# Windowed attention and MLP on one core: one block group of four middle tiles as seven products, with the next batch's casts moved one tile ahead

## Chip, cores and metric

The kernel runs on one core of a Trainium2 chip. The metric is the device time of one execution in microseconds (us), lower is better; it is given as the median of several runs.

## What is computed

There are 8 batches of 8 heads, 576 positions and head dimension 64. Each position attends to the positions at most 32 away; the result goes through a two-layer MLP (512 to 2048 to 512, tanh form of GELU). Inputs and output are float32.

```python
scores = 1/sqrt(64) * q @ k.T          # masked where |i - j| > 32
attn   = softmax(scores)
x      = (attn @ v) as (8 * 576 tokens, 8 heads * 64)
h      = x @ w_in                      # 4608 x 2048
out    = (0.5 * h * (1 + tanh(c * (h + 0.044715 * h**3)))) @ w_out
```

## The kernel before

**Tiles and batches.** The 4608 tokens are worked through in nine tiles of 512 (`t` = 0 to 8, loop at L930). A tile has two parts on TensorE (PE). The *in part* multiplies by `w_in`: 16 blocks of 128 hidden features, each four matmuls of 512 columns (`ffn_in`, L558, matmul L577), and ScalarE (ACT) takes each block through GELU (`gelu`, L583) into `gT`. The *out part* multiplies by `w_out` as seven products of half-size matrices in place of eight (Strassen-Winograd, `ffn_out`, L732, 112 matmuls of 256 columns, L751). The seven products need sums of parts of `gT`, which VectorE (DVE) makes during the in part (`sums`, L686, four instructions for each quarter), and DVE combines the seven results (L762 to L789). Products 0, 2, 4 and 6 share one PSUM bank and products 1, 3 and 5 another, so that product n+2 can start only when the DVE instruction that reads product n has run.

**Attention inside the out part.** While the out part of tile `t` runs, the attention of batch `b = t + 1` is threaded into it. `PLAN` (L46; `PLAN_1` for tile 1) says at which of the 112 matmuls a step is issued: `s` scores of a pair of heads and their exponential, `m` the mask on DVE, `v` the product with the values and the inverse of the sum, `x` the write of the result into `xT`, the transposed MLP input. Group 4 of a batch (its last positions, written -1 for the batch before) uses the "tails" `qt`, `kt`.

**Getting a batch ready.** Queries and keys are loaded in float32 by DMAs that SyncE (SP) issues (`load_qk`, L180: one transfer for q, four for k, two for the tails). DVE casts them to float16 (`turn_queries`, L408, cast L410; `turn_keys`, L416, cast L419; `turn_tails`, L425), and SP issues transposing DMAs into `QT`, `KT` and `KL`. From tile 3 on these casts stand at the head of the in part of the tile in whose out part the batch is attended: batch `t+1` is cast at the beginning of tile `t`, and the loads of batch `t+2` are issued after that. Values go by POOL's queue (`load_v`, L213), released by a one-element copy (L989) that waits for `KL`, and DVE copies them into a second arrangement (`pair_v`, L222).

**The last two tiles.** Tiles 7 and 8 already do two groups of four blocks, named A and B, of their in part as seven products each (`in_product`, L616; matmuls of 256 columns at L629). `in_x` (L606) makes four differences of parts of `xT`, `in_w` (L591) four combinations of `w_in` (once), and `in_mixed` (L632) walks the string `MIX` (L62): a number is a plain block, `A3` or `B3` a product, `s`, `c` and `g` the copy, addition and GELU that follow, `t` and `u` the two halves of `sums`.

**What sets the order.** The order is written out by hand and each engine takes its own instructions in that order. A DVE instruction that waits for data holds back all that follows it on DVE.

The lines that the change and the steps below touch are `PLAN`, `MIX`, `PLAN_1`, the pools of the raw tiles (`rawp`, L109), `load_qk`, `load_tails` (L205), `turn_queries`, `turn_keys`, `turn_tails`, `in_w`, `in_x`, `in_product`, `in_mixed`, `ffn_out` and the main loop.

Of the kernel before, what the change touches and what calls it, by code (L numbers as in the profile page):

```python
# [36 lines left out]
def cut(b):  # L37
# [8 lines left out]
PLAN = {7: "s0@0 s1@1 v-1", 16: "m0 m1 x-1", 33: "s2@0 v0@1 v1", 36: "m2", 44: "x0", 50: "x1",  # L46
        62: "s3@0 s4@1 v2", 66: "m3", 80: "x2", 84: "m4", 91: "v3", 112: "x3"}
# [14 lines left out]
MIX = ("3 g3 A0 s0A B0 s0B 12 g12 A2 B2 cA00 cB00 A1 s1A gA00 A4 B1 s1B gB00 B4 t0 u0 13 g13 A3 s3A B3 s3B 14 g14 "  # L62
       "cA11 cB11 A5 gA10 B5 gB10 gA11 gB11 A6 B6 cA01 cB01 15 gA01 gB01 t1 t2 g15 t3 u1 u2 u3").split()
UNITS = {"A": 1, "B": 2}

PLAN_1 = {12: "s0@0 s1@1 s2", 16: "m0 m1", 36: "m2", 56: "s-1@0 v0@1 v1", 62: "m-1 x0", 64: "x1",
          78: "s3@0 v2 v-1@1", 79: "m3", 88: "x2", 91: "x-1", 97: "v3 s4@1", 112: "x3 m4"}
# [5 lines left out]

RING = 1536
# [4 lines left out]
def kernel(  # L79
# [29 lines left out]
    rawp = ctx.enter_context(tc.tile_pool(name="rawp", bufs=2))  # L109
# [27 lines left out]
    def load_early(b):  # L137


        qr = rawp.tile([128, H, 256], FP32, name="qr")  # L140
        kr = rawp.tile([128, H, 256], FP32, name="kr")
        raws[b] = [qr, kr, None]

        def qk(h0, queues=(nc.sync, nc.sync)):
            for src, dst, queue in zip((q, k), (qr, kr), queues):
                queue.dma_start(
                    dst[:, h0:h0 + 2, :],
                    src[b, h0:h0 + 2, 0:512, :].rearrange("h (p j) d -> p h (j d)", j=4))
# [29 lines left out]
        return qk, tails, vs  # L178

    def load_qk(b):  # L180


        if b == 3:
            qr = raws[3]
        else:
            qr = rawp.tile([128, H, 256], FP32, name="qr")
            load_q(b, qr)
        kr = rawp.tile([128, 4, H, 64], FP32, name="kr")
        if b > 3:
            qt = tailp.tile([16, H, 256], FP32, name="qt", tag="vt")  # L190
            kt = tailp.tile([64, H, 64], FP32, name="kt", tag="tr")
            raws[b] = (qr, kr, qt, kt)
        else:
            raws[b] = [qr, kr, tailp.tile([128, H, 64], FP32, name="tr", tag="tr"), None]
        for c in range(4):
            nc.sync.dma_start(kr[:, c, :, :],
                              k[b, :, 128 * c:128 * c + 128, :].rearrange("h p d -> p h d"))
        load_tails(b, nc.sync)
        if b == 3:
            load_vr(3)  # L200
# [4 lines left out]
    def load_tails(b, queue):  # L205
        if b > 3:
            queue.dma_start(raws[b][2], q[b, :, 512:576, :].rearrange("h (p j) d -> p h (j d)", j=4))
# [194 lines left out]
    def load_vr(b):  # L402
        vr = vrs[b] = rawp.tile([128, 4, H, 64], FP32, name="qr")
# [4 lines left out]
    def turn_queries(b, src, dst, p0, p1):  # L408
# [4 lines left out]
        nc.sync.dma_start_transpose(QTs[b].rearrange("d r j p -> d (r j) p")[:, :, p0:p1],  # L413
                                    dst.rearrange("p r j h d -> p (r j h d)"))

    def turn_keys(b):  # L416
        k16, kr = halfs[b][1], raws[b][1]
        for pr in range(NPAIR):
# [6 lines left out]
    def turn_tails(b):  # L425
        qt, kt = raws[b][2:4]
        qt16 = hp.tile([16, NPAIR, 4, 2, 64], FP16, name="qt16", tag="qt16")
        kt16 = hp.tile([64, NPAIR, 2, 64], FP16, name="kt16", tag="t16")
        turn_queries(b, qt, qt16, 128, 144)
# [4 lines left out]
    def open_and_turn(b):  # L434
        cast_open(b)
        turn_queries(b, raws[b][0], halfs[b][0], 0, 128)
# [154 lines left out]
    def in_w(eng, unit, *which):  # L591
# [14 lines left out]
    def in_x(t):  # L606
# [3 lines left out]
        xc = hp.tile([128, 4, 2, 256], FP16, name="xc", tag="q16" if t % 2 else "k16")  # L610
# [21 lines left out]
    def in_mixed(t):  # L632
        if "A" not in mixed:
            mixed["A"] = rawp.tile([128, 3, 512], FP32, name="sa", tag="qr")
            mixed["B"] = rawp.tile([128, 3, 512], FP32, name="sb", tag="kr")

        place = {"00": (0, "b"), "01": (1, "c"), "11": (2, "c")}
        for step in MIX:
            kind, rest = step[0], step[1:]
            if kind in UNITS:  # L640
                in_product(kind, int(rest))
# [16 lines left out]
            elif kind in "tu":  # L658
                sums(t, int(rest), slice(0, 2) if kind == "t" else slice(2, 4))
# [72 lines left out]
    def ffn_out(t, i):  # L732

        n, blk, f = i // 16, i // 8 % 2, i % 8
        if n == 1 and t >= NT - 2:
            blk, f = divmod(i % 16, 6) if i % 16 < 12 else (i // 2 % 2, 6 + i % 2)
# [28 lines left out]
        elif n == 2:  # L765
            nc.vector.tensor_copy(C11, py)
            if end:
# [162 lines left out]
    for t in range(NT):  # L930
        b = t + 1
        att = b < B
        if t:
# [50 lines left out]
        if t and b + 1 < B:  # L984
            load_qk(b + 1)
        ods = {}
        for i in range(113 if t else 65):
# [8 lines left out]
            for act in plan.get(i, "").split():  # L996
# [61 lines left out]
            if t in (3, 4) and i == 52:  # L1058
                in_w(nc.vector, "B", *((1, 2) if t == 3 else (3, 4)))
# [12 lines left out]
            elif t and i < 112:  # L1072
                ffn_out(t, i)
# [36 lines left out]
```

## Time and profile before

| what | value |
|---|---|
| median of 3 runs | 296.62 us (296.36 to 296.83) |
| the profiled execution | 296.65 us, span 294.6 us |
| PE busy | 285.9 us, 97% of the span |
| DVE busy | 212.4 us, 72% |
| ACT busy | 196.5 us, 67% |
| POOL busy | 88.8 us, 30% |
| tiles 3, 4, 5, 6 (start of one in part to the next) | 30.42, 30.48, 30.42, 30.41 us |
| tiles 7 and 8 (8 to the last matmul) | 26.40, 26.2 us |

The span runs from the first to the last instruction; the time has some 2 us more around it. Busy PE time counts pipelined matmuls, so a full PE is not PE at its peak: the distance from the start of one matmul to the next says more. In a timeline the columns are start, duration, engine, line, operation, output from input with shapes, count, and in square brackets the idle time before the instruction with what ended it.

### The profile page before, as it was taken

What the parts mean: (1) busy time and instruction counts of PE and PEld (TensorE: products, weight loads), DVE (VectorE), ACT (ScalarE), POOL (GpSimd) and SP (SyncE); (2) the same over time, 40 slices, a digit from 0 to 9 for tenths busy, and PEclk for the clock granted to TensorE, in tenths of its full rate; (3) what the DMA queues carried; (4) which work ended last, traced back from release to release, by engine and by line L of the source; (5) the groups of instructions that cost most, each with busy time, mean ns of one, the idle gap of its engine ahead of it and who ended that gap; (6) DMA issues with size and microseconds to landing.
All of it is one profiled execution on the core that took longest, in us unless ns stands there. A gap on an engine that the chain in (4) does not pass through costs nothing.

```text
span 294.6 us, 7286 instructions
## 1 busy us (share of the span) xinstructions
PE 285.9 (97%) x2945; PEld 192.7 (65%) x2945; DVE 212.4 (72%) x467; ACT 196.5 (67%) x315; POOL 88.8 (30%) x143
## 2 busy tenths in 40 slices
PE   8889999999999999999999999999999999999993
PEld 3535545547765687568755885588558867887783
DVE  4755477998897667858796878686957877865762
ACT  5965877777677874787667776796669558706800
POOL 4445335004228713205250615050800050025000
PEclk9999999999999999999999999999999999999998
DMA  7999998999999998999999999899691040004013
GB/s 229 275 380 396 359 305 196 254 186 203 248 229 202 251 202 188 113 139 245 162 212 94 246 157 191 116 245 154 117 190 7 0 118 28 2 26 120 0 47 99
DMA packets 114392, 51.02 MB, mean 173 GB/s; under 512 B 98471, under 2 KB 110247, under 8 KB 114102
## 3 DMA queue, kind: packets, MB, share of 16 engines
q1 hardware_dynamic: 89460, 38.67, 62.4%
q0 software_dynamic: 23776, 10.83, 23.4%
q10 hardware_dynamic: 1122, 1.06, 1.1%
q8 instruction: 23, 0.38, 0.6%
q14 instruction: 11, 0.09, 0.1%
HBM read 36.70 MB, written 9.44 MB: 157 GB/s over the span
## 4 chain that ended last, share of the span: by engine, by line
PE 85%; DVE 5%; DMA 5%; issue 1%; SPq 1%; ACT 1%; POOL 0%; DVEq 0%
PE mm L751 32%; PE ph L577 17%; PE mm L577 16%; PE ps_s L468 4%; PE pu L629 3%; DMA kr<-in_k_dram 3%; PE mm L723 2%; DMA wst<-in_moe_w_in_dram 2%; PE py L723 2%; PE ps_d L495 2%; PE ps_o L505 2%; DVE t L684 2%; DVE s L694 1%; PE mm L629 1%; PE ps_od L495 1%; PE ps_od L505 1%
## 5 line engine op out<-in xcount | busy, mean ns | idle before, releaser
L577 PEld LDWEIGHTS <-w_in 128*128 128x128 f16 x512 | 57.4, 113 | 49.8 <-POOL w_in L250 1.5
L577 PE MATMUL ph<-xT,w_in 128*128 128x512 f16 x256 | 64.5, 379 | 0.6 <-POOL w_in L250 0.6
L577 PE MATMUL mm<-xT,w_in 128*128 128x512 f16 x256 | 64.1, 379 | 0.0
L585 ACT ACTIVATE gT<-mm 128x512 f16<-128x512 f32 x60 | 35.6, 598 | 33.3 <-PE mm L577 32.7
L713 POOL DMA_DIRECT2D out_dram<-y x55 | 32.8, 605 | 82.4 <-DVE y L780 75.3
L751 PEld LDWEIGHTS <-s 128*128 128x128 f16 x512 | 49.3, 98 | 7.1 <-DVE s L694 0.6
L751 PE MATMUL mm<-t,s 128*128 128x256 f16 x376 | 45.2, 273 | 0.2 <-DVE y L764 0.2
L694 DVE TENSOR_TENSOR s<-gT 128x512 f16<-128x512 f16 x64 | 27.5, 430 | 19.1 <-ACT gT L585 18.9
L751 PEld LDWEIGHTS <-gT 128*128 128x128 f16 x384 | 36.2, 98 | 6.4
L585 ACT ACTIVATE gT<-ph 128x512 f16<-128x512 f32 x58 | 32.4, 604 | 10.9 <-PE ph L577 10.9
L481 ACT ACTIVATE pe<-ps_s 128x960 f16<-128x960 f32 (+1 forms) x31 | 29.5, 975 | 13.2 <-PE ps_s L468 13.1
L751 PE MATMUL mm<-w_out,gT 128*128 128x256 f16 x256 | 32.6, 273 | 0.0
L104 ACT ACT_TABLE_LOAD x18 | 23.1, 1283 | 2.2 <-issue 1.9
L530 ACT ACTIVATE lt<-ps_d 128x480 f32<-128x480 f32 (+2 forms) x28 | 15.6, 556 | 10.4 <-PE ps_d L495 6.9
L531 ACT ACTIVATE lt<-lt 128x480 f32<-128x480 f32 (+3 forms) x36 | 21.1, 585 | 1.1
L490 DVE TENSOR_TENSOR pe<-pe,band 128x960 f16<-128x960 f16 x28 | 18.5, 680 | 2.0 <-ACT pe L481 1.9
L505 PEld LDWEIGHTS <-V 128*64 128x64 f16 x520 | 13.7, 111 | 5.5 <-DVE V L226 1.5
L751 PE MATMUL mm<-t,gT 128*128 128x256 f16 x128 | 16.1, 273 | 0.0
L694 DVE TENSOR_TENSOR s<-s,gT 128x512 f16<-128x512 f16 x32 | 14.0, 436 | 1.1
L216 POOL DMA_DIRECT2D V<-in_v_dram x16 | 14.3, 908 | 1.1 <-PE ps_s L468 0.4
L751 PE MATMUL mm<-w_out,s 128*128 128x256 f16 x120 | 14.6, 273 | 0.0
L540 DVE TENSOR_TENSOR xT<-ps_o,lt 128x480 f16<-128x480 f32 (+5 forms) x26 | 13.4, 535 | 1.6 <-PE ps_o L505 1.6
(149 smaller groups left out, 390.3 us busy)
## 6 DMA issues: line engine op xcount, KB each, us to landing
kr<-in_k_dram SPq DMA_DIRECT2D x31, 256.0 KB, 10.2
qr<-in_q_dram SPq DMA_DIRECT2D x6, 1024.0 KB, 5.9
wst<-in_moe_w_in_dram SPq DMA_DIRECT2D x8, 512.0 KB, 6.6
wst<-in_moe_w_out_dram SPq DMA_DIRECT2D x2, 1024.0 KB, 10.5
wst<-in_moe_w_out_dram SPq DMA_DIRECT2D x4, 512.0 KB, 7.4
qr<-in_v_dram SPq DMA_DIRECT2D x8, 256.0 KB, 6.5
V<-in_v_dram POOLq DMA_DIRECT2D x16, 128.0 KB, 8.5
qr<-in_q_dram SPq DMA_DIRECT2D x7, 256.0 KB, 7.3
```

What stands on the lines that cost most here:

```text
L104: nc.scalar.add_instruction(mybir.InstLoadActFuncSet(name=nc.get_next_instruction_name(), act_func_set_id=which, ins=[], outs=[]))
L216: nc.gpsimd.dma_start(V[:, c, :, :], v[b, :, 128 * c:128 * c + 128, :].rearrange("h p d -> p h d"))
L481: nc.scalar.activation(pe, ps[:, :, 0:w], AF.Exp, scale=SCALE)
L490: nc.vector.tensor_tensor(pe, pe, m.rearrange("k (o j) p -> k o j p", o=1).broadcast_to(list(pe.shape)), op=ALU.mult)
L505: nc.tensor.matmul(o[64 * h:64 * h + 64, cols].rearrange("d (j p) -> d j p", j=4)[:, :, p0 - q0:p1 - q0], Vs[b % 2][:, slot, 2 * pr + h, : ...
L530: nc.scalar.activation(lt[:, 0:n], d[:, 0:n], AF.Ln)
L531: nc.scalar.activation(lt[:, 0:n], lt[:, 0:n], AF.Exp, scale=-1.0)
L577: nc.tensor.matmul(ph, w_cols[:, dc, fc // 4, fc % 4, :], xT[:, dc, t * 512 % RING:t * 512 % RING + 512], start=(dc == 0), stop=(dc == 3))
L585: nc.scalar.activation(gTs[t][:, fc, :], phs[fc], AF.Gelu_apprx_tanh)
L694: nc.vector.tensor_tensor(dst, x, y, op=op)
L713: eng.dma_start(out_v[b, j, q0 + p:q0 + p + e, cols], yo[m:m + e, cols])
L751: nc.tensor.matmul(pys["apart"][:, 0:256] if apart else py[:, blk, :], lhsT, wino[w][:, f, :], start=(new and i % (8 if one else 16) == 0) ...
```

## The change

- Tiles 3 to 6 do group B of their in part (blocks 8 to 11) as seven products, by a new string `MIX_1`; the other twelve blocks stay plain. `in_w` for B runs in the in part of tile 2 (before: in the out parts of tiles 3 and 4); `in_x` runs at the head of each tile from 3 on.
- The casts of queries and keys of batch `t+2` move from the head of tile `t+1` into the out part of tile `t` (new steps `a0` to `a3` and `b0` to `b3` in `PLAN`), from tile 2 on. The tails' casts stay in the in part (`f0`, `f1` in `MIX_1`).
- The loads of batch `t+2` are issued inside the in part of tile `t` (step `load`), for batch 4 at block 10 of tile 2.
- In `PLAN`, `v1` moves from 33 to 36; in `PLAN_1`, `v1`, `m-1` and `s4` move; in tile 1 the transposes of the tails move from block 8 to block 6.
- In tiles 7 and 8 the sums S4 of three quarters (`z1 z2 z3`) move from the end of the in part to behind the copy of product 2; the order of product 1 changes; tile 7's last attention group moves from 40 and 66 to 16 and 40; in tile 8 the last four matmuls of product 1 change places with the first four of product 2.
- The raw tiles get fixed buffers in place of rotating ones.

```diff
-PLAN = {7: "s0@0 s1@1 v-1", 16: "m0 m1 x-1", 33: "s2@0 v0@1 v1", 36: "m2", 44: "x0", 50: "x1",
-        62: "s3@0 s4@1 v2", 66: "m3", 80: "x2", 84: "m4", 91: "v3", 112: "x3"}
+PLAN = {7: "s0@0 s1@1 v-1", 16: "m0 m1 x-1", 33: "s2@0 v0@1", 36: "m2 v1", 44: "x0 a0", 50: "x1 a1 a2 a3",
+        62: "s3@0 s4@1 v2 b0 b1", 66: "m3", 80: "x2 b2", 84: "m4 b3", 91: "v3", 112: "x3"}
...
-MIX = ("3 g3 A0 s0A B0 s0B 12 g12 A2 B2 cA00 ...
-       "cA11 cB11 A5 gA10 B5 gB10 gA11 gB11 A6 B6 cA01 cB01 15 gA01 gB01 t1 t2 g15 t3 u1 u2 u3").split()
+MIX = ("3 g3 A0 s0A B0 s0B A2 B2 12 g12 cA00 ...
+       "cA11 cB11 A5 gA10 B5 gB10 gA11 gB11 A6 B6 cA01 cB01 15 gA01 gB01 t1 t2 g15 t3 w1 w2 w3").split()
+MIX_1 = ("f0 3 B0 g3 s0B 4 B2 cB00 B1 s1B load f1 g4 5 g5 6 g6 t0 u0 B3 s3B gB00 pair B4 7 g7 cB11 gB11 12 g12 t1 u1 B5 gB10 B6 cB01 gB01 13 g13 14 g14 t2 u2 15 g15 t3 u3").split()
...
+PARTS = {"t": slice(0, 2), "u": slice(2, 4), "w": slice(2, 3), "z": slice(3, 4)}
+LONE = 3
...
+    def turn_query(b, pr):
+        src, dst = raws[b][0], halfs[b][0]
+        nc.vector.tensor_copy(
+            dst[:, pr, :, :, :].rearrange("p j h d -> p h j d"),
+            src[:, 2 * pr:2 * pr + 2, :].rearrange("p h (j d) -> p h j d", j=4))
+        if pr == NPAIR - 1:
+            nc.sync.dma_start_transpose(QTs[b].rearrange("d r j p -> d (r j) p")[:, :, 0:128],
+                                        dst.rearrange("p r j h d -> p (r j h d)"))
+
+    def turn_keys(b, prs=range(NPAIR)):
...
         if n == 1 and t >= NT - 2:
-            blk, f = divmod(i % 16, 6) if i % 16 < 12 else (i // 2 % 2, 6 + i % 2)
+            blk, f = divmod(i % 16, 4) if i % 16 < 8 else (i // 2 % 2, i // 4 % 4 * 2 + i % 2)
...
         elif n == 2:
             nc.vector.tensor_copy(C11, py)
+            if t >= NT - 2:
+                for step in "z1 z2 z3".split():
+                    sums(t, int(step[1]), PARTS[step[0]])
...
             elif att:
-                if b > 3:
-                    open_and_turn(b)
-                turn_keys(b)
-                if b > 3:
-                    turn_tails(b)
+                if t >= LONE:
+                    in_x(t)
+                if b == 3:
+                    turn_keys(b)
...
-            for fc in range(begun, NF if t < NT - 2 else 0):
+            elif t >= LONE:
+                in_mixed(t)
+            for fc in range(begun, NF if t < LONE else 0):
...
+                if t == 2 and fc == 10:
+                    load_qk(4)
+                if t == LONE - 1 and fc in (8, 9, 10, 11):
+                    in_w(nc.vector, "B", (8, 9, 10, 11).index(fc) + 1)
...
+                elif kind in "ab":
+                    if b + 1 < B:
+                        if kind + str(g) == "a0":
+                            cast_open(b + 1)
+                        turn_query(b + 1, g) if kind == "a" else turn_keys(b + 1, (g,))
...
-                ffn_out(t, i)
+                ffn_out(t, i if t < NT - 1 or not 28 <= i < 36 else i + 4 if i < 32 else i - 4)
```

More of the change, by code (lines that the diff above doesn't have):

```diff
@@ L56 @@
           59: "p0@0 p2@1 x0 x1", 60: "e4 x2 x3", 61: "c1"}
-MIX = ("3 g3 A0 s0A B0 s0B 12 g12 A2 B2 cA00 cB00 A1 s1A gA00 A4 B1 s1B gB00 B4 t0 u0 13 g13 A3 s3A B3 s3B 14 g14 "
-       "cA11 cB11 A5 gA10 B5 gB10 gA11 gB11 A6 B6 cA01 cB01 15 gA01 gB01 t1 t2 g15 t3 u1 u2 u3").split()
+MIX = ("3 g3 A0 s0A B0 s0B A2 B2 12 g12 cA00 cB00 A1 s1A gA00 A4 B1 s1B gB00 B4 t0 u0 13 g13 A3 s3A B3 s3B 14 g14 "
+       "cA11 cB11 A5 gA10 B5 gB10 gA11 gB11 A6 B6 cA01 cB01 15 gA01 gB01 t1 t2 g15 t3 w1 w2 w3").split()
+MIX_1 = ("f0 3 B0 g3 s0B 4 B2 cB00 B1 s1B load f1 g4 5 g5 6 g6 t0 u0 B3 s3B gB00 pair B4 7 g7 cB11 gB11 12 g12 t1 u1 B5 gB10 B6 cB01 gB01 13 g13 14 g14 t2 u2 15 g15 t3 u3").split()
 UNITS = {"A": 1, "B": 2}
-PLAN_1 = {12: "s0@0 s1@1 s2", 16: "m0 m1", 36: "m2", 56: "s-1@0 v0@1 v1", 62: "m-1 x0", 64: "x1",
-          78: "s3@0 v2 v-1@1", 79: "m3", 88: "x2", 91: "x-1", 97: "v3 s4@1", 112: "x3 m4"}
+PARTS = {"t": slice(0, 2), "u": slice(2, 4), "w": slice(2, 3), "z": slice(3, 4)}
+PLAN_1 = {12: "s0@0 s1@1 s2", 16: "m0 m1", 36: "m2", 56: "s-1@0 v0@1", 60: "v1 m-1", 62: "x0", 64: "x1",
+          78: "s3@0 v2 v-1@1", 79: "m3", 88: "x2", 91: "x-1", 97: "v3", 101: "s4@1", 112: "x3 m4"}
 PAIR_1 = {38: slice(0, 4), 50: slice(4, 8)}
@@ L108 @@
     big = ctx.enter_context(tc.tile_pool(name="big", bufs=1))
-    rawp = ctx.enter_context(tc.tile_pool(name="rawp", bufs=2))
+    rawp = ctx.enter_context(tc.tile_pool(name="rawp", bufs=1))
     hp = ctx.enter_context(tc.tile_pool(name="hp", bufs=1))
@@ L137, in load_early @@
     def load_early(b):
-        qr = rawp.tile([128, H, 256], FP32, name="qr")
-        kr = rawp.tile([128, H, 256], FP32, name="kr")
+        qr = rawp.tile([128, H, 256], FP32, name="qr", tag=f"q{b}")
+        kr = rawp.tile([128, H, 256], FP32, name="kr", tag=f"k{b}")
         raws[b] = [qr, kr, None]
@@ L185, in load_qk @@
         else:
-            qr = rawp.tile([128, H, 256], FP32, name="qr")
+            qr = rawp.tile([128, H, 256], FP32, name="qr", tag="q0")
             load_q(b, qr)
-        kr = rawp.tile([128, 4, H, 64], FP32, name="kr")
+        kr = rawp.tile([128, 4, H, 64], FP32, name="kr", tag="k1" if b == 3 else "k0")
         if b > 3:
-            qt = tailp.tile([16, H, 256], FP32, name="qt", tag="vt")
-            kt = tailp.tile([64, H, 64], FP32, name="kt", tag="tr")
-            raws[b] = (qr, kr, qt, kt)
+            raws[b] = [qr, kr]
         else:
@@ L197, in load_qk @@
                               k[b, :, 128 * c:128 * c + 128, :].rearrange("h p d -> p h d"))
-        load_tails(b, nc.sync)
+        if b < 5:
+            load_tails(b, nc.sync)
         if b == 3:
@@ L206, in load_tails @@
         if b > 3:
+            raws[b] += [tailp.tile([16, H, 256], FP32, name="qt", tag="vt"),
+                        tailp.tile([64, H, 64], FP32, name="kt", tag="tr")]
             queue.dma_start(raws[b][2], q[b, :, 512:576, :].rearrange("h (p j) d -> p h (j d)", j=4))
@@ L402, in load_vr @@
     def load_vr(b):
-        vr = vrs[b] = rawp.tile([128, 4, H, 64], FP32, name="qr")
+        vr = vrs[b] = rawp.tile([128, 4, H, 64], FP32, name="vr", tag="q1")
         for c in range(4):
@@ L406, in load_vr, with turn_queries @@
                               v[b, :, 128 * c:128 * c + 128, :].rearrange("h p d -> p h d"))
-    def turn_queries(b, src, dst, p0, p1):
+    def turn_queries(b):
+        src = raws[b][2]
+        dst = hp.tile([16, NPAIR, 4, 2, 64], FP16, name="qt16", tag="qt16")
         for pr in range(NPAIR):
@@ L412, in turn_queries @@
                 src[:, 2 * pr:2 * pr + 2, :].rearrange("p h (j d) -> p h j d", j=4))
-        nc.sync.dma_start_transpose(QTs[b].rearrange("d r j p -> d (r j) p")[:, :, p0:p1],
+        nc.sync.dma_start_transpose(QTs[b].rearrange("d r j p -> d (r j) p")[:, :, 128:144],
                                     dst.rearrange("p r j h d -> p (r j h d)"))
-    def turn_keys(b):
+    def turn_query(b, pr):
[7 more added lines that the diff above has]
+    def turn_keys(b, prs=range(NPAIR)):
         k16, kr = halfs[b][1], raws[b][1]
-        for pr in range(NPAIR):
+        for pr in prs:
             nc.vector.tensor_copy(k16[:, pr, :, :, :], kr[:, :, 2 * pr:2 * pr + 2, :])
@@ L423, in turn_keys, with turn_key_tails @@
                     k16[:, pr - 1:pr + 1, :, :, :].rearrange("p r c h d -> p (r c h d)"))
-    def turn_tails(b):
-        qt, kt = raws[b][2:4]
-        qt16 = hp.tile([16, NPAIR, 4, 2, 64], FP16, name="qt16", tag="qt16")
+    def turn_key_tails(b):
+        kt = raws[b][3]
         kt16 = hp.tile([64, NPAIR, 2, 64], FP16, name="kt16", tag="t16")
-        turn_queries(b, qt, qt16, 128, 144)
         nc.vector.tensor_copy(kt16.rearrange("p r h d -> p (r h d)"), kt.rearrange("p h d -> p (h d)"))
@@ L435, in open_and_turn @@
         cast_open(b)
-        turn_queries(b, raws[b][0], halfs[b][0], 0, 128)
+        for pr in range(NPAIR):
+            turn_query(b, pr)
     groups = {}
@@ L595, in in_w @@
         if (unit, "s") not in mixed:
-            halves = [(rawp if unit == "A" else yp).tile([128, 2, 2, 2, 128], FP16, name="wc" + unit + str(x),
-                                                         tag=("qr", "kr")[x] if unit == "A" else "yo") for x in range(2)]
-            mixed[unit, "s"] = [half[:, x] for half in halves for x in range(2)]
+            if unit == "A":
+                wc = rawp.tile([128, 4, 2, 2, 128], FP16, name="wcA", tag="q0")
+                mixed[unit, "s"] = [wc[:, x] for x in range(4)]
+            else:
+                mixed["xw"] = rawp.tile([128, 2, 4, 2, 256], FP16, name="xw", tag="k1")
+                mixed[unit, "s"] = [mixed["xw"][:, 1, x].rearrange("p d (h c) -> p d h c", h=2) for x in range(4)]
         S1, S2, S3, S4 = mixed[unit, "s"]
@@ L609, in in_x @@
         B11, B12, B21, B22 = (xT[:, d:d + 2, pos + c:pos + c + 256] for d in (0, 2) for c in (0, 256))
-        xc = hp.tile([128, 4, 2, 256], FP16, name="xc", tag="q16" if t % 2 else "k16")
+        xc = mixed["xw"][:, 0] if t < NT - 2 else \
+            hp.tile([128, 4, 2, 256], FP16, name="xc", tag="q16" if t % 2 else "k16")
         T1, T2, T3, T4 = (xc[:, x] for x in range(4))
@@ L614, in in_x, with in_product @@
             nc.vector.tensor_tensor(dst, a, b, op=ALU.subtract)
-    def in_product(unit, n):
+    def in_product(unit, n, alone):
         a, w, new = WINO[n]
         if n == 0:
-            phs[unit, "a"] = psO.tile([128, 512], FP32, name="pu", tag="O") if unit == "A" else bank(1)
+            phs[unit, "a"] = psO.tile([128, 512], FP32, name="pu", tag="O") if unit == "A" or alone else bank(1)
         elif n in (2, 4):
             which = "b" if n == 2 else "c"
-            if unit == "A":
+            if unit == "A" or alone:
                 phs[which] = psS.tile([128, 2, 512], FP32, name="pu2", tag="S1" if n == 2 else "S0")
@@ L632, in in_mixed @@
     def in_mixed(t):
-        if "A" not in mixed:
-            mixed["A"] = rawp.tile([128, 3, 512], FP32, name="sa", tag="qr")
-            mixed["B"] = rawp.tile([128, 3, 512], FP32, name="sb", tag="kr")
+        if "B" not in mixed:
+            mixed["B"] = rawp.tile([128, 3, 512], FP32, name="sb", tag="q1")
+        if t == NT - 2:
+            mixed["A"] = rawp.tile([128, 3, 512], FP32, name="sa", tag="k0")
         place = {"00": (0, "b"), "01": (1, "c"), "11": (2, "c")}
-        for step in MIX:
+        for step in MIX if t >= NT - 2 else MIX_1:
             kind, rest = step[0], step[1:]
-            if kind in UNITS:
-                in_product(kind, int(rest))
+            if step == "pair":
+                pair_v(t + 1, nc.vector.tensor_copy)
+            elif step == "load":
+                if t + 2 < B:
+                    load_qk(t + 2)
+            elif step == "f0":
+                turn_queries(t + 1)
+            elif step == "f1":
+                turn_key_tails(t + 1)
+                if t + 2 < B:
+                    load_tails(t + 2, nc.sync)
+            elif kind in UNITS:
+                in_product(kind, int(rest), t < NT - 2)
             elif kind == "s":
@@ L657, in in_mixed @@
                 nc.scalar.activation(gTs[t][:, fc, :], phs[fc], AF.Gelu_apprx_tanh)
-            elif kind in "tu":
-                sums(t, int(rest), slice(0, 2) if kind == "t" else slice(2, 4))
+            elif kind in PARTS:
+                sums(t, int(rest), PARTS[kind])
             else:
@@ L958 @@
                     nc.sync.dma_start(raws[2][4], v[2, :, 512:S, :].rearrange("h p d -> p h d"))
-                    raws[3] = rawp.tile([128, H, 256], FP32, name="qr")
+                    raws[3] = rawp.tile([128, H, 256], FP32, name="qr", tag="q0")
                     load_q(3, raws[3])
@@ L963 @@
                     cast_v(2, fc - 6)
+                if t == 1 and fc == 6:
+                    trans_tails(1, psO.tile([128, 8, 128], FP16, name="pt", tag="O"))
                 if t == 1 and fc == 8:
-                    trans_tails(1, psO.tile([128, 8, 128], FP16, name="pt", tag="O"))
                     cast_tails(2, nc.scalar.copy)
@@ L974 @@
                                 copy_q=nc.scalar.copy)
-                if t > 1 and fc == 8 and att:
+                if t == 2 and fc == 8:
                     pair_v(b, nc.vector.tensor_copy)
-        plan = PLAN_0 if not t else PLAN_1 if t == 1 else PLAN if att else {40: "v-1", 66: "x-1"} if t == B - 1 else {}
+                if t == 2 and fc == 10:
+                    load_qk(4)
+                if t == LONE - 1 and fc in (8, 9, 10, 11):
+                    in_w(nc.vector, "B", (8, 9, 10, 11).index(fc) + 1)
+        plan = PLAN_0 if not t else PLAN_1 if t == 1 else PLAN if att else {16: "v-1", 40: "x-1"} if t == B - 1 else {}
         def group(g):
@@ L983 @@
             load_table(exp_set)
-        if t and b + 1 < B:
+        if t == 1:
             load_qk(b + 1)
@@ L1057 @@
                 in_x(t + 1)
-            if t in (3, 4) and i == 52:
-                in_w(nc.vector, "B", *((1, 2) if t == 3 else (3, 4)))
             if t == NT - 3 and i in (52, 86):
```

## Prediction

> **What bounds the kernel now.** I read the page's busy line and the chain of waits first, then the table of windows by tile, then the timelines of PE, DVE and SP around the places that the change touches. The busy line and the engine shares of the chain:
>
> ```profile
> PE 285.9 (97%) x2945; PEld 192.7 (65%) x2945; DVE 212.4 (72%) x467; ACT 196.5 (67%) x315; POOL 88.8 (30%) x143
> PE 85%; DVE 5%; DMA 5%; issue 1%; SPq 1%; ACT 1%; POOL 0%; DVEq 0%
> ```
>
> PE is the bound, and from tile 3 to 6 it never idles (30.42 busy of 30.42 us in the windows). So there a change is worth what it takes from PE, unless something newly makes PE wait. Two lines of the chain, of a plain in part and of tile 8's products (start, duration, what, count):
>
> ```profile
> 154.72 1.73 PE mm L577 x8
> ...
> 269.13 1.75 PE pu L629 x16
> ```
>
> A 512-column matmul costs 0.216 us from start to start, a 256-column one 0.109.
>
> **Seven products, tiles 3 to 6.** Removed for each tile: 4 blocks x 4 matmuls x 0.216 = 3.45 us. Added: 7 products x 4 x 0.109 = 3.06. Gain 0.39 a tile, **1.6 us** in four.
> A rule of the Trainium skill speaks against it: "TensorE: Matmul & The Clock Gate", section "Back-to-back issue gap", gives 81 ns sustained for 128 columns and 131 for 512; between them 256 columns would be some 98 (an estimate), and 28 x 98 against 16 x 131 ns would lose 0.65 us a tile, 2.6 in all. The rows above measure both shapes in this kernel and decide.
>
> What comes with it lies on DVE and ACT. DVE in the in part gains `in_x` (1.5 us in tile 7, 238.11 to 239.65), one copy and three additions of 0.6 each, 3.9 us, and loses the query and key casts, 1.47 + 1.49: net 0.9, against 3.1 us in which DVE idled there in tile 4 (0.62 + 0.62 + 1.90 before the sums). ACT gains two copies of 0.58 against some 3 us of idle between GELUs (0.27 each). Without these covers the 0.9 and 1.2 us would delay the sums or GELUs by as much a tile. The product's bank is read by DVE between B0 and B1 (0.7 us, with block 4 and B2, 1.3 us of PE, between): no wait. I cost them at nothing.
>
> **Casts in the out part, tiles 3 to 5.** Eight casts of 0.37 us join DVE. The tight place is ahead of L771, which product 5 waits for. In tile 4 there stood 1.2 us of `in_w` and 0.39 idle; now a0 to b1, 6 x 0.37 = 2.2. L771 ends 0.6 later, at 171.9, and product 5 begins at 172.18: 0.3 us left. Nothing again, at most 0.2 a tile. On SP, QT and KT now go before the loads, KL behind q and k; KL is first needed by `s4`, values a tile later. In tile 4 of before, loads issued at 131.23 were cast at 146.8 and 148.3 without a wait, 17.1 us for k at most; now they are issued some 5.8 us into the in part and k is cast at 24.1, 18.3 us later: on time, with little proved slack.
>
> **Tile 2 is different.** Its out part now casts batch 4, a whole in part sooner, but its loads do not go out sooner: SP issues back to back. SP and DVE in tiles 2 and 3 (start, duration, engine, line), and the landing of the k transfers issued from 95.5 on:
>
> ```profile
> 93.67 2.14 SPq L203 DMA_DIRECT2D qr<-in_q_dram  x1
> 95.86 13.13 SPq L196 DMA_DIRECT2D kr<-in_k_dram  x4
> 109.09 3.01 SPq L207 DMA_DIRECT2D qt<-in_q_dram  x1
> ```
>
> ```profile
> L196 SPq DMA_DIRECT2D kr<-in_k_dram x4: 1109/3064/5760, 95.9 to 106.6; - x4
> ...
> DMA to landing us min/median/max: 12.7/12.7/12.7
> ```
>
> ```profile
> 106.27 0.66 DVE L540 TENSOR_TENSOR xT<-ps_od,lt 128x480 f16<-128x480 f32 x1 [0.44 <-ACT lt L531]
> 106.89 0.69 DVE L766 COPY y<-mm 128x512 f32<-128x512 f32 x1
> 107.49 0.65 DVE L540 TENSOR_TENSOR xT<-ps_o,lt 128x480 f16<-128x480 f32 x1
> 109.80 0.69 DVE L771 TENSOR_TENSOR y<-mm,y 128x512 f32<-128x512 f32 x1 [1.66 <-PE mm L751]
> ...
> 118.00 1.57 DVE L419 CAST k<-kr 128x512 f16<-128x512 f32 x4
> ```
>
> `kr` is issued in four parts, the last at 106.6 (SP is not idle from 49 us to there, and the changed kernel's SP order up to these loads is the same). Emitting `load_qk(4)` at block 10 moves it past nothing on SP. The third part, issued at 102.8, lands 12.7 later, at 115.5; each k cast reads all four parts. The fourth lands after that and no later than 118.0, where the cast began without a recorded wait. In the new order b0 stands after x1 and a1 to a3, at about 109.2 (108.1 + 3 x 0.37), and waits on DVE until k lands. Behind it are queued b1, L771, m3, L774, x2, and for L771 waits product 5:
>
> ```profile
> 109.37 2.14 PE L751 MATMUL mm<-t,s 128*128 128x256 f16 x18
> 111.34 1.36 PE L751 MATMUL mm<-t,gT 128*128 128x256 f16 x11
> ```
>
> Product 5 started at 111.34. Now it starts at landing + 2 x 0.37 + 0.69. For the landing I take 117.2, near the 118.0 row, a little less because the output stores that ran beside it from 114.95 now come later. 117.2 + 1.43 = 118.6: **PE waits 7.3 us** (5.6 to 8.1 by the two rows). q is no such case: a0 stands at 106.9, and casting q is at most some 0.5 late.
>
> PE then also loses its clock. After the last matmul (290.0) the granted clock fell:
>
> ```profile
> 290.00:294.60 4.60, 0.00 (x0) 0.00 (x0) 0.42 (x1) 0.00 (x0) 0.00 (x0) 0.81 0.39 104
> ```
>
> 0.81 (the eighth column) in 4.6 us means half speed for 1.75, so it fell 2.85 us after the last matmul. A wait of 7.3 is longer. The way back is seen at the start:
>
> ```profile
> 1.26 3.59 PE L288 MATMUL spin<-KT 128*128 128x512 f16 x8 [1.26 <-DVE KT L283]
> 4.65 0.62 PE L382 MATMUL pt<-idn,q 128*128 128x128 f16 x4
> ```
>
> Eight matmuls in 3.39 us, 0.424 each, where 8 x 0.216 = 1.73 would do: **1.7 us lost** on resuming. Bounds: 0 (clock kept) to 3.4 (twice that slow stretch); I take the row.
>
> **Tail, tiles 7 and 8.** In tile 8, L764 stood behind six S3 and S4 sums, and product 3 behind L764:
>
> ```profile
> 282.09 0.68 DVE L764 TENSOR_TENSOR y<-mm,y 128x512 f32<-128x512 f32 x1
> ...
> 282.83 1.36 PE L751 MATMUL mm<-t,s 128*128 128x256 f16 x11 [0.17 <-DVE y L764]
> ```
>
> Products 0 to 2 took 276.96 to 282.83, 5.87 us; 48 x 0.109 are 5.23. Three sums fewer (1.0 us) ahead of L764 and the new order of product 1 (which spent 1.95 instead of 1.75 waiting for sums) leave 0.1: gain 0.5. Late next is the S3 sum before L771, done long before. Tile 7 had 1.95 for product 1 too and 0.1 at product 3, and its attention step now gives the sums 0.45 more: gain 0.3. Together **0.8** (0.3 to 1.2). Tile 1 had PE waits of 0.36 (L356 for L360) and 0.15 (`s4`) that the new places remove; since tile 2 waits for an absolute landing, those 0.5 are swallowed.
>
> **Sum**, against the profiled execution's 296.65 us (0.03 above the median, so nothing to correct): 296.65 - 1.6 - 0.8 + 7.3 + 1.7 = **303.3 us**, slower.
>
> **Rivals.**
> 1. *k lands in time* (0.13), ending faster. The mechanism is the queue of loads ahead of batch 4's keys in tile 2. L771 is on time if k lands by 109.9 (111.34 - 1.43); from 112.3 on the delay eats the 2.4 us of gains. Against it: k lay behind POOL's value loads and stores, DMA share 1.30 in that out part, and landed after 115.5. For it: loads without company are quicker, and a small shift could part them. Then 296.65 - 1.6 - 0.8 - 0.5 = 293.8.
> 2. *Half a delay* (0.04): k at 112 to 114, wait 2 to 4 us, clock kept: 296.3 to 298.5.
> 3. *DVE becomes the bound as well* (0.08): the 0.3 us ahead of L771 and 2.2 in the in part do not hold; 0.5 us in each of four tiles: 305.3.
> 4. *Later batches are late too* (0.04): 18.3 us do not suffice in tiles 3 to 5; 2 us each: 309.3.
>
> The forecast has 0.71. Its own range: 299.5 (landing 115.5, clock kept, larger tail gain) to 306.5 (118.0, clock 3.4, small gains). Rival 3 lies inside, rival 2 at its lower edge; 298.5 to 306.5 holds some 8 in 10. About 0.2% is what a measurement of this kernel tells from no change: faster 0.15 (rival 1 and a part of 2), same 0.02, slower 0.83.
>
> **What would show it.** Right: in tile 2, DVE idle of 7 to 9 us before the first L419-type cast, released by the DMA into `kr`, PE idle of 7 us before product 5, matmuls at half speed after it, a PEclk digit under 9 there. Tiles 3 to 6 at 30.0 us each, 26.1 and 25.7 for tiles 7 and 8. Wrong: no DVE wait for `kr` in tile 2 (rival 1), such waits in tiles 3 to 5 (rival 4), PE waits for DVE at L771 or at bank changes of the in part (rival 3), or 256-column matmuls slower than 0.109.

## The result and the profile after

The changed kernel took 306.86 us (median of 6 runs, 304.99 to 307.73) against 296.78 for the kernel before (6 runs beside it). The ratio is 1.0323, 95% interval 1.0288 to 1.0359: slower by 3.2%. The forecast was 303.3 us (299.5 to 306.5). On its scale the ratio gives 306.2 us (1.0323 x 296.62), at the upper edge of the range; the median itself lies 0.4 us beyond it. The profiled execution took 307.17 us, span 305.1. An execution over 1.5% longer than the shortest of its kernel counts as a slow one and is left out of the ratios, not of the medians, and the profiled executions of `tail_late` (311.55 us) and `stores_first` (303.42 us) are such.

The busy line and the engine shares of the chain, for the changed kernel. PE lost 3 points of its span, and in the chain two shares grew: DMA from 5 to 8%, SP's queue from 1 to 7%.

```profile
PE 287.5 (94%) x2993; PEld 198.2 (65%) x2993; DVE 227.2 (74%) x499; ACT 197.0 (65%) x323; POOL 87.7 (29%) x143
PE 82%; DMA 8%; SPq 7%; DVE 1%; issue 0%; POOL 0%; ACT 0%; ACTq 0%; DVEq 0%
```

The table of windows, one for each of tiles 2 to 8 of the changed kernel (stretch, length, PE, PEld, DVE, ACT and POOL busy, granted clock, DMA share, GB/s):

```profile
84.64:127.98 43.34, 33.42 (x337) 22.20 (x335) 27.07 (x55) 23.23 (x36) 14.72 (x23) 0.88 1.13 185
127.98:158.22 30.24, 30.24 (x344) 22.08 (x343) 26.04 (x57) 21.69 (x35) 9.24 (x14) 1.00 0.96 167
158.22:188.53 30.31, 30.31 (x345) 22.09 (x344) 26.49 (x61) 21.83 (x36) 10.33 (x17) 1.00 1.02 171
188.53:218.79 30.26, 30.26 (x345) 22.05 (x343) 26.38 (x57) 21.72 (x36) 10.00 (x16) 1.00 1.08 167
218.79:249.03 30.24, 30.24 (x344) 22.08 (x343) 25.68 (x53) 21.74 (x36) 5.24 (x10) 1.00 0.25 55
249.03:275.00 25.97, 25.97 (x213) 20.59 (x212) 19.22 (x42) 14.33 (x25) 4.53 (x9) 1.00 0.15 42
275.00:300.64 25.64, 25.64 (x202) 20.21 (x200) 16.45 (x34) 10.77 (x20) 5.21 (x10) 1.00 0.22 64
```

The same tiles took 30.74, 30.42, 30.48, 30.41, 30.42, 26.40 and 26.34 us before. Tile 2 alone lost 12.60 us; tiles 3 to 6 gained 0.68 together, tile 7 0.43 and tile 8 0.70. Tile 1 gained 0.45, and the first tiles started 0.32 later. That adds up to the 10.66 us between the two last matmuls (289.98 and 300.64).

Inside tile 2, the timelines of DVE and PE, and the chain of waits with SP's issues of the keys (start, duration, what; entries of 0.04 us between the lines are left out):

```profile
108.67 0.42 DVE L424 CAST q<-qr 128x512 f16<-128x512 f32 x1
...
110.16 1.09 DVE L424 CAST q<-qr 128x512 f16<-128x512 f32 x3
120.18 0.76 DVE L434 CAST k<-kr 128x512 f16<-128x512 f32 x2 [8.93 <-DMA kr<-in_k_dram]
120.86 0.68 DVE L804 TENSOR_TENSOR y<-mm,y 128x512 f32<-128x512 f32 x1
```

```profile
111.42 2.14 PE L781 MATMUL mm<-t,s 128*128 128x256 f16 x18
121.59 2.51 PE L781 MATMUL mm<-t,gT 128*128 128x256 f16 x11 [8.03 <-DVE y L804]
```

```profile
97.69 2.89 SPq L197
100.63 4.56 SPq L197
105.23 3.07 SPq L197
108.35 11.71 DMA kr<-in_k_dram
...
120.94 0.61 DVE y L804
121.59 2.51 PE mm L781 x11
```

L434 and L804 are L419 and L771 of the kernel before. The first key cast stands in DVE's queue at 111.2 and waits 8.9 us for the fourth part of the keys, issued at 108.35 and landed at 120.06. Behind it stands the y sum, and behind that product 5, which began at 111.34 before and now begins at 121.59.

What followed the wait is seen in the granted clock, the third column from the end:

```profile
113.40:121.59 8.19, 0.16 (x2) 0.00 (x0) 1.41 (x4) 0.18 (x1) 0.00 (x0) 0.67 1.19 160
121.59:123.50 1.91, 1.91 (x10) 1.31 (x10) 1.91 (x4) 0.00 (x0) 0.00 (x0) 0.50 0.92 180
123.50:125.50 2.00, 2.00 (x22) 1.18 (x21) 0.91 (x3) 0.79 (x2) 0.00 (x0) 0.50 0.00 1
125.50:127.98 2.48, 2.48 (x21) 2.02 (x19) 1.26 (x2) 1.67 (x2) 0.74 (x2) 0.81 0.56 106
127.98:130.00 2.02, 2.02 (x12) 1.10 (x11) 1.79 (x6) 0.00 (x0) 2.02 (x5) 1.00 0.67 201
```

From product 5 to the end of the tile PE took 6.39 us instead of 4.17: 2.2 us went to the clock.

Not foreseen was a second wait in tile 2: PE stood 1.88 us at 96.9 for the cast of batch 3's tails (L355), which lay on POOL behind eight output stores of tile 1, and these behind the casts of batch 3's values (PE's row, then POOL's):

```profile
98.77 0.40 PE L360 MATMUL pt<-idn,t 128*128 128x128 f16 x4 [1.88 <-POOL t L355]
```

```profile
92.75 0.62 POOL L1032 CAST V<-vr 128x512 f16<-128x512 f32 x1 [0.68 <-DMA vr<-in_v_dram]
93.31 2.39 POOL L743 DMA_DIRECT2D out_dram<-y  x4
95.68 0.68 POOL L741 DMA_DIRECT2D out_dram<-y  x1
96.36 1.67 POOL L743 DMA_DIRECT2D out_dram<-y  x3
98.02 0.69 POOL L355 CAST t<-tr 128x512 f16<-128x512 f32 x1
```

In the kernel before, the same stores went out two us earlier:

```profile
91.28 2.13 POOL L713 DMA_DIRECT2D out_dram<-y  x4
93.39 0.68 POOL L711 DMA_DIRECT2D out_dram<-y  x1
94.07 2.21 POOL L713 DMA_DIRECT2D out_dram<-y  x3
```

### The profile page after: what moved, and what is told of

The parts are those of the page before. It is cut to its first block, busy times and chain, and to the rows that moved or that the text cites. A ratio compares the mean times of both kernels' runs of the same rounds, so it can differ in the third digit from the quotient of the medians.

```text
span 305.1 us, 7435 instructions
## 1 busy us (share of the span) xinstructions
PE 287.5 (94%) x2993; PEld 198.2 (65%) x2993; DVE 227.2 (74%) x499; ACT 197.0 (65%) x323; POOL 87.7 (29%) x143
## 3 DMA queue, kind: packets, MB, share of 16 engines
q0 software_dynamic: 23776, 10.83, 22.4%
## 4 chain that ended last, share of the span: by engine, by line
PE 82%; DMA 8%; SPq 7%; DVE 1%; issue 0%; POOL 0%; ACT 0%; ACTq 0%; DVEq 0%
PE mm L781 30%; PE ph L591 16%; PE mm L591 13%; PE pu L647 7%; DMA kr<-in_k_dram 4%; SPq L197 3%; PE ps_s L482 3%; PE py L753 2%; PE mm L753 2%; PE ps_d L509 2%; DMA wst<-in_moe_w_in_dram 2%; PE ps_o L519 2%; DMA qr<-in_q_dram 1%; SPq L275 1%; PE mm L647 1%; PE ps_od L509 1%
## 5 line engine op out<-in xcount | busy, mean ns | idle before, releaser
L591 PEld LDWEIGHTS <-w_in 128*128 128x128 f16 x448 | 50.2, 113 | 39.6 <-POOL w_in L254 1.3
L591 PE MATMUL ph<-xT,w_in 128*128 128x512 f16 x240 | 60.4, 379 | 0.6 <-POOL w_in L254 0.6
L743 POOL DMA_DIRECT2D out_dram<-y x55 | 30.8, 568 | 86.7 <-DVE y L813 79.4
L591 PE MATMUL mm<-xT,w_in 128*128 128x512 f16 x208 | 53.7, 379 | 0.0
L599 ACT ACTIVATE gT<-mm 128x512 f16<-128x512 f32 x28 | 16.5, 599 | 27.6 <-PE mm L591 27.4
L781 PE MATMUL mm<-w_out,gT 128*128 128x256 f16 x256 | 33.5, 273 | 0.0
L724 DVE TENSOR_TENSOR s<-gT 128x512 f16<-128x512 f16 x64 | 26.5, 419 | 8.1 <-ACT gT L599 4.4
L781 PE MATMUL mm<-t,gT 128*128 128x256 f16 x128 | 17.8, 291 | 8.0 <-DVE y L804 8.0
L599 ACT ACTIVATE gT<-ph 128x512 f16<-128x512 f32 x38 | 20.9, 605 | 6.6 <-PE ph L591 6.6
L687 ACT ACTIVATE gT<-ph 128x512 f16<-128x512 f32 x22 | 13.2, 600 | 4.8 <-PE ph L591 4.7
L434 DVE CAST k<-kr 128x512 f16<-128x512 f32 x24 | 9.3, 423 | 8.9 <-DMA kr<-in_k_dram 8.9
```

The source lines that it names most:

```text
L591: nc.tensor.matmul(ph, w_cols[:, dc, fc // 4, fc % 4, :], xT[:, dc, t * 512 % RING:t * 512 % RING + 512], start=(dc == 0), stop=(dc == 3))
L599: nc.scalar.activation(gTs[t][:, fc, :], phs[fc], AF.Gelu_apprx_tanh)
L724: nc.vector.tensor_tensor(dst, x, y, op=op)
L743: eng.dma_start(out_v[b, j, q0 + p:q0 + p + e, cols], yo[m:m + e, cols])
L781: nc.tensor.matmul(pys["apart"][:, 0:256] if apart else py[:, blk, :], lhsT, wino[w][:, f, :], start=(new and i % (8 if one else 16) == 0) ...
```

## The experiments

All ratios are to runs of the kernel before on the same chip in the same job (medians there 297.67, 298.36 and 297.82). Times in the expectations are on the scale of the first result.

**1. The early key casts alone, in the kernel before** (`keys4_early_alone`; shortened, the opening of batch 4's buffers moves along):

```
+            if t == 2 and i in (62, 80, 84):
+                if i == 62: cast_open(4)
+                turn_keys(4, {62: (0, 1), 80: (2,), 84: (3,)}[i])
...
-                turn_keys(b)              # head of tile 3
+                if b != 4: turn_keys(b)
```

> The kernel before, with one thing of the change alone: batch 4's key casts at blocks 62, 80 and 84 of tile 2's out part. Theory A: the keys landed at 117.9 us in the trace of before; product 5 then starts at 117.9 + 2 x 0.37 + 0.69 = 119.4 instead of 111.3, so PE waits 8.0 us, and the matmuls after the wait lose another 2 us of clock, as in the changed kernel: 296.8 + 8.0 + 2.0 = 306.8 us, 305.5 to 308. Rival B: less than half of it comes from the casts alone, under 301.8 us.

Measured: 307.06 us, ratio 1.030 (1.0232 to 1.0369). DVE and PE of this kernel in tile 2:

```profile
117.25 0.76 DVE L419 CAST k<-kr 128x512 f16<-128x512 f32 x2 [8.61 <-DMA kr<-in_k_dram]
117.92 0.68 DVE L772 TENSOR_TENSOR y<-mm,y 128x512 f32<-128x512 f32 x1
```

```profile
118.66 2.50 PE L752 MATMUL mm<-t,gT 128*128 128x256 f16 x11 [6.66 <-DVE y L772]
```

Four casts moved up in an otherwise unchanged kernel give a loss of the same size. The keys landed at 117.1 here, product 5 began 1.5 us later, and the granted clock was 0.50 for some 3.7 us after it. In the two traces tile 2 ends 9.0 us later than before here and 12.5 in the changed kernel, which has its keys later and gains 1.8 us in tiles 3 to 8. Theory A holds, rival B falls.

**2. The key casts taken back, in the changed kernel** (`keys4_late`; shortened):

```
-                if b == 3:
+                if b in (3, 4):
                     turn_keys(b)          # behind in_x, head of the in part
...
-  turn_keys(b + 1, (g,))                  # plan steps b0 to b3
+  if b > 3: turn_keys(b + 1, (g,))
```

> The changed kernel, but batch 4's four key casts stand behind in_x at the head of tile 3 instead of in tile 2's out part; the query casts stay where the change put them. Theory A (key casts of batch 4 hold DVE until their load lands, nothing else in the move costs anything): tile 2's out part falls from 27.2 us to about 16.8 us, the key wait goes to the head of tile 3, where it is at most 1 to 2 us of DVE and hidden by PE's first blocks; the 1.9 us that PE waits in tile 2 for the cast of the tails stays and now counts. 306.9 - 10.4 = 296.5 us, 295.9 to 297.5. Rival B (DVE, POOL and SP are crowded in tile 2 by the whole change): tile 2 stays at least 3 us longer than the 30.7 us of before beyond the tail wait, 299 us or more.

Measured: 297.79 us, ratio 0.999 (0.9964 to 1.0016). Tiles 2 and 3 of this kernel:

```profile
84.90:117.07 32.17, 31.05 (x337) 21.15 (x336) 25.22 (x52) 23.17 (x36) 14.31 (x22) 1.00 1.28 216
117.07:148.25 31.18, 30.59 (x345) 22.12 (x343) 27.33 (x61) 21.76 (x36) 9.54 (x15) 1.00 1.06 172
```

Tile 2 is 11.2 us shorter than in the changed kernel (43.34), though the keys still landed at 119.2: at the head of tile 3 DVE reached them at 119.4. The 1.1 us between length and PE busy in tile 2 is the wait for the tails; in tile 3, 0.6 us is lost since the copy of product B0 stands behind the casts. These two, and the longer out parts of experiment 3, use up what the other parts gain: this version only draws level.

**3. v1 beside v0 again** (`v1_back`): `33: "s2@0 v0@1 v1", 36: "m2"` in the plan of the changed kernel.

> The changed kernel, but v1 stands at block 33 beside v0 again instead of block 36. Theory C (the three w_out products between v0 and v1 cost PE one more switch between products and attention): the out parts of tiles 3 to 6 fall from 16.82 to 16.60 us each, 0.9 us in four tiles; the same 0.2 in tile 2 is swallowed by the wait for the keys. 306.9 - 0.9 = 306.0 us. Rival D (v1 was moved because its operands are late at block 33, with the new casts on DVE): a wait for DVE or ACT appears ahead of v1's matmuls and takes the 0.2 us a tile or more: 306.9 us or above.

Measured: 305.71 us, ratio 1.0254 (1.0217 to 1.0292), against 1.0323 for the changed kernel. Tiles 3 to 6 took 30.02, 30.15, 30.02 and 30.02 us, without a new wait: 0.84 us less than the 121.05 of the changed kernel, where 0.9 was forecast. Theory C holds. The rest of the distance between the two traces lies in tile 2, 2.0 us shorter here (41.31 us): the keys landed at 118.9; whether v1 has a part in that was not tested. How v1 costs is seen in tile 6, before and after (PE, start and duration; v0's last matmuls, then v1's first):

```profile
226.00 0.40 PE L505 MATMUL ps_od<-pe,V 128*64 128x96 f16 x14
226.23 0.37 PE L495 MATMUL ps_d<-pe,ones 128*64 128x480 f16 x2
226.43 0.40 PE L505 MATMUL ps_o<-pe,V 128*64 128x96 f16 x14
```

```profile
237.57 0.40 PE L519 MATMUL ps_od<-pe,V 128*64 128x96 f16 x14
237.90 0.50 PE L781 MATMUL mm<-w_out,gT 128*128 128x256 f16 x3
238.33 0.39 PE L509 MATMUL ps_d<-pe,ones 128*64 128x480 f16 x2
```

Side by side, v0's fourteen small matmuls pass to v1 after 0.23 us. With three 256-column matmuls between them they take 0.33, and the three take 0.43 where 3 x 0.109 are 0.33: one switch more, 0.2 us.

**4. The tails' transposes two blocks later** (`tail_late`): `t == 2 and fc == 13` became `fc == 15`.

> The changed kernel, but the transposes of batch 3's tails stand two blocks later (after block 15 of tile 2's in part), so that PE does not wait 1.9 us for POOL's cast. Theory A with an absolute landing: PE comes to product 5 some 1.9 us earlier and waits there 1.9 us longer (9.9 instead of 8.0); the end stays at 306.9 us, within 0.5. Rival E (the delays of tile 2 add, because the key loads are issued in step with the engines): 305.0 us.

Measured: 307.47 us, ratio 1.0218 (1.014 to 1.0295). The ratio rests on two of six runs (302.71 and 306.49 us); its interval holds rival E's 1.027 and not theory A's 1.032, while the median of all six fits theory A: inconclusive. Its trace shows that the wait for the tails was gone and another stood in its place: a y sum waited 4.3 us on DVE for the landing of tile 1's output stores, whose buffer it writes, and PE 2.7 us for the sum. So the stores became suspect for the keys as well.

**5. Tile 1's stores ahead of the value casts on POOL** (`stores_first`; shortened), in the changed kernel:

```
-            if t == 1 and i == 94:
-                for c in range(4): nc.gpsimd.tensor_copy(Vs[1][:, c, :, :], vrs[3][:, c, :, :])
...
             ffn_last(t)
+            if t == 1:
+                for c in range(4): nc.gpsimd.tensor_copy(Vs[1][:, c, :, :], vrs[3][:, c, :, :])
```

> The changed kernel with one edit on POOL's queue alone: the four casts of batch 3's values stand behind tile 1's output stores instead of ahead of them. The early key casts stay in tile 2's out part. In best_head, which has the same edit, the stores were issued at 83.7 to 89.1 us instead of 93.3 to 98.0, and batch 4's keys landed at 114.2 us instead of 120.1. Theory A (tile 2 ends at the landing of the keys plus 1.4 us, and the landing is late because the stores lie ahead of the keys in the transfers): product 5 starts at 114.2 + 1.4 = 115.6 instead of 121.6, so 6 us of the loss go, and PE, which comes at some 111.7 without the wait for the tails, waits 4 us; the clock is still lost after it. 306.9 - 6 = 300.9 us, 299.9 to 302; 1.014 of before. Rival F (the landing does not depend on the stores, and was early in best_head because the key casts of tile 2 no longer held the engines): product 5 starts within 1 us of 121.6, 306 us or above.

Measured: 302.11 us (297.71 to 303.99), ratio 1.009 (1.0046 to 1.0133), below the forecast 1.014; the quotient of the two medians is 1.014. POOL, DVE and PE of this kernel:

```profile
83.99 2.26 POOL L743 DMA_DIRECT2D out_dram<-y  x4 [0.83 <-DVE y L813]
...
90.05 0.53 POOL L743 DMA_DIRECT2D out_dram<-y  x1 [1.17 <-DMA V<-in_v_dram]
```

```profile
115.99 0.76 DVE L434 CAST k<-kr 128x512 f16<-128x512 f32 x2 [6.38 <-DMA kr<-in_k_dram]
```

```profile
117.40 2.51 PE L781 MATMUL mm<-t,gT 128*128 128x256 f16 x11 [5.49 <-DVE y L804]
```

With the key casts where the change put them, moving only the stores brought the landing from 120.1 to 115.9 and product 5 from 121.59 to 117.40, 4.2 us where 6 were forecast. Product 5 follows the landing, and the landing follows the stores; rival F falls. The twelve traces agree on the second: from SP's first key issue to the landing of the last key part it took 20.7 to 24.9 us in the six with the stores behind the value casts (the kernel before, the changed kernel, experiments 1 to 4), and 16.7 to 17.5 in the six with the stores ahead (this one and the five below). The wait for the tails is gone too. The three shortest runs here (297.7 to 299.3 us) have a mean granted clock of 0.996 or 0.997, the changed kernel's six 0.981 to 0.987, so the half clock in tile 2 was probably short or absent in them; that is not shown, as no trace of one was kept.

**6. A better version, and what the other parts are worth.** `best_head` has experiments 2, 3 and 5 together:

> The changed kernel with three edits: batch 4's key casts at the head of tile 3 (as in keys4_late), v1 beside v0 again (as in v1_back), and the four POOL casts of batch 3's values behind tile 1's output stores in POOL's queue instead of ahead of them. Theory: the stores no longer wait for the value loads, so neither the cast of the tails (1.1 us of PE wait in keys4_late) nor the y sum that waits for the stores' landing (2.7 us in tail_late) is late in tile 2; with 0.22 us a tile from v1 in five tiles this gives 1.1 + 1.1 = 2.2 us below keys4_late, which stood at 0.999 of before: 0.992 of before, some 294.4 us for a before of 296.8. Rival: another DMA that lands late takes the tail's place (the stores now stand ahead of the transposes and value loads in the transfer backlog): 0.996 or above.

Measured: 295.92 us, ratio 0.9937 (0.9900 to 0.9974), faster than both kernels. The interval holds the theory's 0.992 and the rival's 0.996. The keys landed at 114.2, before DVE asked for them. Its tiles 2 to 4:

```profile
84.76:115.40 30.64, 30.64 (x337) 21.24 (x336) 25.23 (x52) 23.00 (x36) 13.56 (x21) 1.00 1.32 232
115.40:146.64 31.24, 30.51 (x345) 22.05 (x343) 28.06 (x61) 21.82 (x36) 9.62 (x15) 1.00 1.01 166
146.64:176.76 30.12, 30.12 (x344) 22.09 (x343) 26.31 (x61) 21.77 (x35) 10.38 (x17) 1.00 1.28 194
```

Tile 2 is whole again; 1.1 us remain in tile 3, where DVE is busy 28.1 of 31.2 us.

`best_mid` and `best_f0` tried to get these by moving casts further into tile 3's in part (the keys and the query tail behind product B1; the query tail alone behind it):

> As best_head, but batch 4's key casts and the query tail's casts stand after product B1 in tile 3's in part, just before the loads of batch 5, instead of ahead of the in part. In keys4_late tile 3 took 31.2 us, 1.0 more than the next tile, with a PE wait of 0.5 us for the copy of product B0. Theory: that goes, 0.8 us below best_head, 0.989 of before. Rival: the keys' transposes then come too late for the first scores of tile 3's out part, and PE waits there: equal to best_head or slower.

> As best_head, but in tile 3 alone the four casts of the query tail (1.4 us of DVE) stand after product B1, so that the copy of product B0 comes straight behind the key casts. In best_head that copy began at 120.53, 1.2 us after B0 was done at 119.3, and product B2 waited 0.67 us for it. Theory: B2 starts on time, tile 3's in part takes 13.4 instead of 14.1 us: 0.7 us below best_head, 0.991 of before. Rival: what stands behind the casts now (sums, the second addition, the transposes of the query tail) is late instead, as in best_mid: equal to best_head or slower.

Measured: 0.9966 (0.9937 to 0.9995) and 0.9944 (0.9916 to 0.9971). Neither is below `best_head`, and the forecast gains of 0.8 and 0.7 us did not come. In `best_mid` PE waited 1.9 us for a product's addition behind eight casts, in `best_f0` 0.6 us for the same addition behind four. In each of the three orders tried, a copy or an addition stands behind the casts.

> As best_head, but tiles 3 to 6 compute all sixteen blocks plainly (64 matmuls of 512 columns), without in_x, the bank copies and the additions. Theory: what the seven products save is 0.39 us a tile, as in the in parts of the two traces (13.42 against 13.81), and the casts in the out part cost nothing: 1.6 us more than best_head. Rival: the additions, copies and in_x cost DVE and ACT time that shows on PE: equal to best_head or faster.

`plain_blocks` drops the seven products in tiles 3 to 6 from `best_head`: 0.9975 (0.9946 to 1.0004), some 1.1 us more than `best_head`, where 1.6 was forecast. Its tile 4 took 30.48 us against 30.12 above. The theory's direction and size fit, though the two intervals overlap; the trace is the sharper measure.

> As best_mid, but in tiles 7 and 8 everything that the change reordered stands as in the kernel before: the MIX order, the last halves of sums 1 to 3, the order inside product 1, the swap in the last tile, and the attention step of tile 7. Theory: 1.1 us more than best_mid, as the two traces say from the start of tile 7 to the last matmul (52.74 us before, 51.61 after). By the prediction's working it would be 0.8. Rival: part of the 1.1 is due to the seven products' side effects (buffers, clock) and stays: 0.5 us or less.

`tail_undone` takes back the order of tiles 7 and 8 from `best_mid`: 1.0003 (0.9972 to 1.0033), 1.1 us more. Tiles 7 and 8 (to the start of the last matmul), here and in `best_mid`:

```profile
240.10:266.50 26.40, 26.36 (x212) 20.50 (x211) 19.14 (x42) 14.54 (x25) 4.53 (x9) 1.00 0.15 41
266.50:292.56 26.06, 25.85 (x201) 20.13 (x200) 16.28 (x34) 10.88 (x20) 5.21 (x10) 1.00 0.21 61
```

```profile
239.92:265.89 25.97, 25.97 (x213) 20.59 (x211) 19.23 (x42) 14.32 (x25) 4.53 (x9) 1.00 0.15 42
265.89:291.26 25.37, 25.37 (x201) 20.19 (x200) 16.45 (x34) 10.77 (x20) 5.21 (x10) 1.00 0.22 63
```

1.12 us, all of it from the new order.

## Why the prediction was right, and where its sizes were off

The profiled execution lost 10.5 us where the sum had 6.6. By its terms, on the last matmul's 10.66:

- **Tile 2's wait, +7.3 forecast, +10.25 measured** (product 5 at 121.59 instead of 111.34). The mechanism is the one forecast, link by link: experiment 1 shows that the casts alone are enough for it, experiment 2 that without them it is gone. The term that was mis-sized is the landing: "I take 117.2, near the 118.0 row, a little less because the output stores that ran beside it from 114.95 now come later". It was 120.06, 2.9 us later. The order of SP's issues was the same, as assumed, but not their times: the first key part was issued 1.8 us later than before (97.69 instead of 95.86). From there it took 22.4 us instead of 22.0, so the little less did not come; in `keys4_early_alone` it took 20.7 us (landing 117.1). The stores that move the landing by 4 to 5 us are others, tile 1's, issued 20 us earlier (experiment 5). Why SP came 1.8 us later is known only in part. Its issues stand back to back, and its lag grew from 0.6 us at 45 us to 0.9 at 72 and 1.7 at 82; the DMA engines, over nine tenths busy in most slices from 55 us on, may have left it little room to catch up. The first cause stays open.
- **The clock, +1.7 forecast, +2.2 measured.** It was 1.7 in `keys4_early_alone` and 2.6 in `stores_first` (5.82 and 6.75 us from product 5 to the tile's end, against 4.17). The Trainium skill, "TensorE: Matmul & The Clock Gate", section "What's actually happening", says that the array falls to half clock after an idle window of about 3.4 us and takes as long to come back. The traces agree roughly on the fall, and the way back could be longer: in the five with a wait of 5.5 to 8.3 us for the keys, the granted clock fell to 0.50 between 2.7 and 4.6 us after the last matmul and stayed there for 3.3 to 6.1 us after the first one behind the wait. Through the 1.9 us wait for the tails it stayed 1.00. So the single figure taken from the start of the kernel was one of a spread.
- **Seven products, -1.6 forecast, -0.68 measured.** The in parts went from 13.81 to 13.42 us, the 0.39 a tile of the working; the gaps that the Trainium skill, "TensorE: Matmul & The Clock Gate", section "Back-to-back issue gap", gives, by which it would have been a loss, do not hold here. What failed is a part that was not costed: the plan's step v1 went three products further on, and the out parts grew from 16.60 to some 16.83, 0.22 in each of four tiles. The prediction costs no step that moved for its switches on PE.
- **The casts in the out part of tiles 3 to 5, nothing forecast, nothing measured:** 16.82, 16.89 and 16.84 us against 16.83 in tile 6, which has none.
- **Tail, -0.8 forecast, -1.13 measured.** The out parts gave 0.28 and 0.55, as worked out (0.3 and 0.5); the new order of the in parts gave another 0.15 in each tile (13.32 to 13.18), which had been costed at nothing.
- **Tile 1, 0.5 gained and swallowed:** 0.45, swallowed. So was the unforeseen 1.9 us for the tails, by the same argument: where an absolute landing sets the end, time gained or lost ahead of it does not count. That is read from the chain, in which from 93.65 us to the landing only SP's issues and the transfer stand, and not PE's wait at 96.9; experiment 4 did not decide it. With the keys out of the way it counts in full, as `keys4_late` shows.

Of the rivals, 1 and 2 fall with the 8.9 us that DVE idled; 3 with the list of PE's waits, which names no sum after tile 2; 4 with tiles 3 to 5, 30.2 to 30.3 us each.

That the time still lies in the stated range is in part luck. The landing of 120.06 is beyond the range's own bound of 118.0; at the upper edge this was made up for by a clock loss of 2.2 us, where the edge had taken 3.4.

## What to carry to other kernels

A wait moved into an engine's in-order queue costs everything behind it: before a cast is moved up, compare the time at which it will stand at the head of its queue with the landing of the last transfer that it reads, not with the moment at which the load was issued. Where the DMA engines are near full, as here, that landing can depend on what was issued long before on another queue: eight stores moved it by 4 to 5 us, and no key cast had to move for it. And count switches on PE when a small step is moved, not only the engine that feeds it.

## What the runs showed of the hardware

- Eight output stores sent 7 to 9 us earlier (84 to 90.6 instead of 93.3 to 98.0) made loads on another queue, whose issue began no earlier (at 98.4 instead of 97.7), land 4.2 us earlier; their issue was done at 106.5 instead of 110.8. `best_head` beside `keys4_late`, which differ in v1 as well, shows the same (stores from 83.7 instead of 92.8, landing at 114.2 instead of 119.2).
- Loads in parts do not land evenly: the four key parts of the changed kernel landed at 110.6, 113.4, 117.3 and 120.1, though each took SP 2.4 to 4.6 us to issue; the last one needed 11.7 us from its issue.
- Three 256-column matmuls put between two groups of small attention matmuls cost 0.22 us a tile beyond their own 0.33, by the length of the out parts.
